# A channel product as seven products of block sums, with converted weights kept in DRAM

## The chip, the cores and the metric

The kernel runs on one core of a Trainium2 chip. Its time is the device time of one execution in microseconds (us). The engines are named as the profile names them: PE is TensorE's matmuls and PEld its weight loads, DVE is VectorE, ACT ScalarE, POOL GpSimd, SP SyncE. Each engine works through its own instructions in the order in which they are written; they wait for each other by semaphores.

## What is computed

```python
# attention with decay, 4 batches x 8 heads x 768 x 64, then a mixer
x = attn_out.transpose(0, 2, 1, 3).reshape(4, 768, 512)
h = relu(x.transpose(0, 2, 1) @ w_tok1) @ w_tok2       # tokens: 768 -> 256 -> 768
u = x + h.transpose(0, 2, 1)
out = u + relu(u @ w_ch1) @ w_ch2                      # channels: 512 -> 1536 -> 512
```

The mixer's weights come as 64-bit floats and are turned into 32-bit ones on the chip, by integer operations on the two words of each number. The change concerns the last line, `u @ w_ch1`, and what comes around it.

## The kernel before

*Attention stage (to some 185 us).* Sixteen pairs of heads run through a software pipeline; the mixer's token products are filled in between as "groups" (`token_hidden`, a tile `ph` of 18 matmuls, and `token_out`, a tile `pu` of 6), with weight conversions in the gaps. The result `u` lies transposed in SBUF, channels on partitions: 4 channel tiles by 3072 tokens.

*Channel stage.* The 3072 tokens are 6 blocks `k` of 512; the 1536 hidden channels are 6 groups `g` of 256. A unit is one (g, k). Each operand is split in a high and a low half of a reduced 32-bit format (`uh`/`ul`, `c1h`/`c1l`, `c2h`/`c2l`, `hh`/`hl`), and a product is three matmuls: high by high, low by high, high by low. `mm1` makes a hidden tile of 128 x 512 in PSUM from 4 channel tiles, 12 matmuls of 128x128 by 128x512 (L613). ACT takes its ReLU as the high half `hh` (L617), DVE subtracts for the low half `hl` (L618). `mm2` multiplies the two hidden tiles of a unit by the second weights, 6 matmuls for each of 4 output tiles (L634), and DVE adds the tile to `u` in place (L637). `mm2` runs one unit behind `mm1`, so PE alternates between the two. The blocks of `u` are split once, in the first six units (ACT L510, POOL L511).

*Order of the work.* It is written out by hand, instruction by instruction, for all five engines; no scheduler moves it. Small steps that fill gaps stand in a list `waiting`, and `later(n)` takes the next n of it. The conversion of a piece of weights (`narrow`) is such a list: an absolute value on ACT (L350), five steps on DVE (L351, L354, L357, L360, L363), a cast of the high half on ACT (L345), a subtraction of the low half on POOL (L346). A group has four pieces of 128x512. Group g+1 is loaded and converted during the six units of group g, one piece a unit.

PSUM has 8 banks: tag `sc` 4, `xT` 1, `sh` 3. At the end the last block is transposed by PE (L657) and written by two queues; the others by DVE (L644) and SP.

Of the kernel before, what the change touches and what calls it, by code (L numbers as in the profile page):

```python
# [21 lines left out]
def kernel(  # L22
# [310 lines left out]

    def narrow(raw, a, sg, hi, lo, view):

        low, high = raw[:, :, 0], raw[:, :, 1]
        af = a.bitcast(F32)

        def split():
            nc.scalar.copy(out=hi, in_=view(af))  # L345
            nc.gpsimd.tensor_sub(out=lo, in0=view(af), in1=hi.bitcast(F32))  # L346

        waiting.extend(
            [
                lambda: nc.scalar.activation(af, high.bitcast(F32), AF.Abs),  # L350
                lambda: nc.vector.tensor_scalar(  # L351
                    out=sg, in0=high, scalar1=0x80000000, scalar2=None, op0=ALU.bitwise_and
                ),
                lambda: nc.vector.scalar_tensor_tensor(  # L354
                    out=sg, in0=low, scalar=29, in1=sg, op0=ALU.logical_shift_right, op1=ALU.bitwise_or
                ),
                lambda: nc.vector.tensor_scalar(  # L357
                    out=af, in0=af, scalar1=HIGH_MIN, scalar2=HIGH_MAX, op0=ALU.max, op1=ALU.min
                ),
                lambda: nc.vector.tensor_scalar(  # L360
                    out=a, in0=a, scalar1=3, scalar2=0x40000000, op0=ALU.logical_shift_left, op1=ALU.bitwise_xor
                ),
                lambda: nc.vector.scalar_tensor_tensor(  # L363
                    out=a, in0=a, scalar=0x7FFFFFFF, in1=sg, op0=ALU.bitwise_and, op1=ALU.bitwise_or
                ),
                split,
            ]
        )
# [365 lines left out]
```

## Time and profile before

| | |
|---|---|
| median of 3 runs | 602.48 us (600.57 to 603.64) |
| profiled execution | 604.87 us, its span 603.1 us |
| granted TensorE clock, mean | 0.993 |
| matmuls | 3854, of which 864 in `mm1` and 864 in `mm2` |
| DRAM | read 34.61 MB, written 6.29 MB |

The span is counted from the first to the last instruction; what lies outside it (1.8 us here) is start and end of the execution. Busy time of an engine is time with an instruction in it; for PE, matmuls overlap each other, so that the length shown for one is more than the step from one to the next. A row of the groups reads: line, engine, operation, output <- inputs, shapes, xcount | busy us, mean ns of one | idle time of the engine ahead of it, and what ended it. The rows themselves stand in the prediction.

### The profile page before, as it was taken

The numbers are of one execution on the slowest core, as the hardware profiler recorded it, in microseconds if no ns is written. First come the engines' busy times: TensorE is split into PE (matmuls) and PEld (weight loads), VectorE is DVE, ScalarE is ACT, GpSimd is POOL, SyncE is SP. The second block draws the span as 40 slices with busy tenths as digits, with TensorE's granted clock in tenths as the row PEclk, the third lists the DMA queues.
The fourth block names the chain that finished last, engine by engine and source line by source line (L and its number), as shares of the span: only waits on it lengthen the run. The fifth ranks groups of instructions, "written<-read, shape, count | busy, mean of one in ns | idle before, by whom it ended". The sixth has DMA issues, their size and how long they took to land.

```text
span 603.1 us, 9441 instructions
## 1 busy us (share of the span) xinstructions
PE 581.8 (96%) x3854; PEld 493.9 (82%) x3854; DVE 327.0 (54%) x574; ACT 147.0 (24%) x283; POOL 162.0 (27%) x147
## 2 busy tenths in 40 slices
PE   5978899999999999999999999999999999999996
PEld 4877899989988878888888888888888888888885
DVE  4569867685552356635554356345553564445653
ACT  3344423343323123312121122111120121101101
POOL 6848655567613335400000011000010010000000
PEclk9979999999999999999999999999999999999999
DMA  9999696665101001100210101001110010006566
GB/s 185 242 226 168 103 189 134 136 115 92 30 34 36 2 35 36 41 30 36 69 36 0 36 35 38 33 1 65 41 35 1 35 36 1 1 4 101 83 102 130
DMA packets 142314, 41.50 MB, mean 69 GB/s; under 512 B 135104, under 2 KB 136640, under 8 KB 142272
## 3 DMA queue, kind: packets, MB, share of 16 engines
q1 hardware_dynamic: 141072, 40.12, 31.7%
q10 hardware_dynamic: 1200, 0.79, 0.4%
q8 instruction: 30, 0.49, 0.4%
q14 instruction: 12, 0.10, 0.1%
HBM read 34.61 MB, written 6.29 MB: 68 GB/s over the span
## 4 chain that ended last, share of the span: by engine, by line
PE 89%; DVE 5%; DMA 2%; ACT 2%; issue 1%; SPq 0%; DVEq 0%; ACTq 0%
PE ph L613 33%; PE po L634 33%; PE ph L419 6%; PE pu L439 5%; PE xT L285 3%; PE sc L261 3%; PE xT L295 2%; DMA uT<-in_moe_w_tok_dram 2%; PE kt L186 2%; PE kv L228 1%; PE xp L317 1%; DVE uT L354 1%; DMA qn<-in_q_dram 1%; DVE xlo L326 1%; DVE a L270 1%
## 5 line engine op out<-in xcount | busy, mean ns | idle before, releaser
L618 DVE SCALAR_TENSOR_TENSOR hl<-ph,hh 128x512 fp32r<-128x512 f32 x72 | 49.8, 692 | 189.5 <-ACT hh L617 189.5
L617 ACT ACTIVATE hh<-ph 128x512 fp32r<-128x512 f32 x72 | 43.1, 599 | 288.8 <-PE po L634 221.4
L613 PE MATMUL ph<-ul,c1h 128*128 128x512 f32 x288 | 113.4, 394 | 0.0
L613 PE MATMUL ph<-uh,c1l 128*128 128x512 f32 x288 | 113.2, 393 | 0.0
L613 PE MATMUL ph<-uh,c1h 128*128 128x512 f32 x288 | 113.1, 393 | 0.0
L634 PE MATMUL po<-hh,c2l 128*128 128x512 f32 x288 | 112.8, 392 | 0.0
L634 PE MATMUL po<-hh,c2h 128*128 128x512 f32 x288 | 112.8, 392 | 0.0
L634 PE MATMUL po<-hl,c2h 128*128 128x512 f32 x288 | 112.0, 389 | 0.0
L637 DVE TENSOR_TENSOR uT<-po,uT 128x512 f32<-128x512 f32 x144 | 95.7, 683 | 8.3 <-PE po L634 8.0
L613 PEld LDWEIGHTS ph<-ul,c1h 128*128 128x128 f32 x288 | 54.1, 188 | 12.3
L613 PEld LDWEIGHTS ph<-uh,c1h 128*128 128x128 f32 x288 | 54.2, 188 | 12.1
L634 PEld LDWEIGHTS po<-hh,c2h 128*128 128x128 f32 x288 | 54.0, 188 | 12.1
L634 PEld LDWEIGHTS po<-hl,c2h 128*128 128x128 f32 x288 | 54.1, 188 | 11.9
L613 PEld LDWEIGHTS ph<-uh,c1l 128*128 128x128 f32 x288 | 54.0, 188 | 11.9
L634 PEld LDWEIGHTS po<-hh,c2l 128*128 128x128 f32 x288 | 54.1, 188 | 11.5
L346 POOL TENSOR_TENSOR c1l<-wa,c1h 128x512 fp32r<-128x512 f32 x10 | 13.0, 1298 | 159.7 <-ACT c1h L345 159.7
L285 PE MATMUL xT<-a,vn 128*64 128x128 f32 x384 | 37.1, 285 | 6.3 <-ACT uT L302 6.3
L511 POOL TENSOR_TENSOR ul<-uT,uh 128x512 fp32r<-128x512 f32 x24 | 32.2, 1372 | 38.4 <-ACT uh L510 38.4
L346 POOL TENSOR_TENSOR c2l<-wa,c2h 128x512 fp32r<-128x512 f32 x10 | 13.0, 1302 | 91.7 <-ACT c2h L345 62.0
L210 POOL TENSOR_SCALAR kd<-kn,mask 128x320 f32<-128x320 f32 x32 | 36.5, 1151 | 1.3
L270 DVE TENSOR_TENSOR a<-sc,mask 128x384 f32<-128x384 f32 x64 | 31.3, 549 | 5.8 <-PE sc L261 5.6
L249 POOL COPY stb<-sv 64x320 f32<-64x320 f32 x32 | 26.1, 814 | 26.8 <-DVE sv L236 25.9
(76 smaller groups left out, 783.3 us busy)
## 6 DMA issues: line engine op xcount, KB each, us to landing
raw<-in_moe_w_ch_dram SPq DMA_DIRECT2D x20, 512.0 KB, 3.6
kn<-in_k_dram SPq DMA_DIRECT2D x32, 192.0 KB, 3.8
vn<-in_v_dram SPq DMA_DIRECT2D x16, 384.0 KB, 5.0
out_dram<-y SPq DMA_DIRECT2D x80, 64.0 KB, 2.0
qn<-in_q_dram SPq DMA_DIRECT2D x44, 96.0 KB, 3.8
uT<-in_moe_w_tok_dram SPq DMA_DIRECT2D x2, 1536.0 KB, 8.6
uT<-in_moe_w_ch_dram SPq DMA_DIRECT2D x4, 512.0 KB, 4.6
qn<-in_q_dram SPq DMA_DIRECT2D x10, 192.0 KB, 4.5
```

What stands on the lines that cost most here:

```text
L210: nc.gpsimd.tensor_scalar_mul(kds[i][:, h], loaded[i][0][:, 0 : NC - 1, h], mask[:, 2 * p + h, P - 1 : P])
L249: nc.gpsimd.tensor_copy(out=st[r, :, h, :], in_=sv[r].rearrange("p (e c) -> p c e", c=NC - 1))
L270: nc.vector.tensor_mul(out=a, in0=sc[h].rearrange("p (c i) -> p c i", i=P), in1=mask[:, 2 * p + h, None, :].broadcast_to([P, 3, P]),)
L285: nc.tensor.matmul(out=xT[h * D : (h + 1) * D, cs], lhsT=vns[i][:, h, c, :], rhs=weights_of[i, g, h][:, cg, :], start=(cg == 0), stop=False,)
L419: nc.tensor.matmul(out=ph, lhsT=w[:, c, fs], rhs=x[:, c], start=(i == 0), stop=(i == 3 * NC - 1))
L439: nc.tensor.matmul(out=pu, lhsT=h[:, kk, cs], rhs=w[:, kk, ss], start=(i == 0), stop=(i == 3 * NK - 1))
L511: nc.gpsimd.tensor_sub(out=two(ul[:, t]), in0=ub, in1=two(uh[:, t]).bitcast(F32))
L613: nc.tensor.matmul(out=ph, lhsT=w[:, ct, js], rhs=x[:, ct], start=(i == 0), stop=(i == 11))
L617: nc.scalar.activation(hh, ph, AF.Relu)
L618: nc.vector.scalar_tensor_tensor(out=hl, in0=ph, scalar=0.0, in1=hh.bitcast(F32), op0=ALU.max, op1=ALU.subtract)
L634: nc.tensor.matmul(out=po, lhsT=w[:, jj, cs], rhs=h, start=(i == 0), stop=(i == 3 * JG - 1))
L637: nc.vector.tensor_add(out=ub, in0=two(po), in1=ub)
```

## The change

`u @ w_ch1` is done for pairs of blocks by Winograd's form of the 2x2 scheme: token blocks 2r and 2r+1 (top, bot), the two halves of the 512 input channels, and the two halves of a group's 256 hidden channels make eight products of 128-wide hidden tiles, which become seven products of sums. A *quad* n is a pair r and a group g: n = 6r + g, so the channel stage is three passes (r = 0, 1, 2) over the six groups, 18 quads.

- Weights: `combine` builds four sums of the converted quarters on POOL, then splits seven operands in halves (ACT `high`, POOL `low`), the last four as one operation of 128x1024.
- Tokens: three operands are plain (`raw_operand`: 1, 2, 3), four are sums (`make` on DVE, `part` splits them on ACT and POOL or DVE: 6, 7, 5, 4). For the first pass operands 1 and 2 are made in the attention stage, the others in quad 0, each right ahead of its product. For later passes they are made in the last quad of the pass before, after the old operand's last product.
- Products (`PROD`: order 1, 2, 6, 7, 5, 3, 4, six matmuls each) accumulate into three banks `a`, `b`, `d`. Bank `b` collects products 1, 6, 5, 3, and ACT takes snapshots of it on the way (`snap`); DVE adds a snapshot to `a` or `d` (`whole`), and `relu` takes the sum. In the first five quads three of four ReLUs go the "slow" way: a second ReLU in place on ACT, and the subtraction on POOL instead of DVE.
- `mm2` of quad n-1 is done between the products of quad n, one output tile after each of six products and two after the seventh; it now uses the `sh` banks. In quad 0 the remaining ten token groups take that place; the units used to mix with the last ones of these.
- Group g+1 is converted during quad g of the first pass (four pieces in one quad). The converted halves are written to DRAM (`keep_c1`, `keep_c2`, SP queue) and fetched for passes 1 and 2, the first weights a quad ahead, the second in the quad itself, a quad ahead of their `mm2`.
- The last block to finish is 4, not 5.

```diff
@@ weights of a group
+        return [
+            lambda: eng.tensor_add(out=s1, in0=a0[:, :, 1], in1=a1[:, :, 1]),
+            raw0,
+            lambda: eng.tensor_sub(out=s2, in0=s1, in1=a0[:, :, 0]),
+            lambda: eng.tensor_sub(out=s3, in0=a0[:, :, 0], in1=a0[:, :, 1]),
+            raw1,
+            lambda: eng.tensor_sub(out=s4, in0=a1[:, :, 0], in1=s2),
+            sums,
+        ]
...
+    PROD = (1, 2, 6, 7, 5, 3, 4)
+    WI = {1: 0, 2: 1, 4: 2, 5: 3, 6: 4, 7: 5, 3: 6}
...
+    def halve(r, o, ct, src, eng):
+        oh, ol = ops[r, o]
+        nc.scalar.copy(out=two(oh[:, ct]), in_=src)
+        eng.tensor_sub(out=two(ol[:, ct]), in0=src, in1=two(oh[:, ct]).bitcast(F32))
...
+        terms = {
+            1: lambda ct: (block(bot, ct), block(top, ct)),
+            2: lambda ct: (block(bot, 2 + ct), two(tt[1][:, ct])),
+            3: lambda ct: (block(bot, 2 + ct), block(bot, ct)),
+            4: lambda ct: (block(top, 2 + ct), two(tt[2][:, ct])),
+        }
...
+            6: [
+                lambda: make(1, 0, V),
+                lambda: make(1, 1, V),
+                lambda: make(2, 0, V),
+                lambda: part(6, 2, 0, G),
+                lambda: make(2, 1, V),
+                lambda: part(6, 2, 1, V),
+            ],
+            7: [lambda: make(3, 0, V), lambda: part(7, 3, 0, G), lambda: make(3, 1, V), lambda: part(7, 3, 1, V)],
+            5: [lambda: part(5, 1, 0, G), lambda: part(5, 1, 1, V)],
+            3: raw_operand(r, 3, ob, G),
+            4: [lambda: make(4, 0, V), lambda: part(4, 4, 0, G), lambda: make(4, 1, V), lambda: part(4, 4, 1, V)],
...
+        nc.scalar.activation(hh, src, AF.Relu)
+        if slow:
+            nc.scalar.activation(src, src, AF.Relu)
+            nc.gpsimd.tensor_sub(out=hl, in0=src, in1=hh.bitcast(F32))
...
@@ mm1, now product(n, s)
+        into = {1: "b", 2: "a", 6: "b", 7: "d", 5: "b", 3: "b", 4: "d"}[o]
...
-        for ct in range(4):
-            for w, x in ((c1h, uh), (c1l, uh), (c1h, ul)):
-                nc.tensor.matmul(out=ph, lhsT=w[:, ct, js], rhs=x[:, ct], start=(i == 0), stop=(i == 11))
+        for ct in range(2):
+            for w, x in ((ch, oh), (cl, oh), (ch, ol)):
+                nc.tensor.matmul(
+                    out=c[into], lhsT=w[:, WI[o], ct], rhs=x[:, ct], start=(first and i == 0), stop=(i == 5),
...
+        slow = r == 0 and g < NG - 1
...
+        if o == 1:
+            snap("p1")
+        elif o == 2:
+            relu(n, 0, 0, whole("a", "p1"), slow)
+        elif o == 6:
+            snap("u2")
+        elif o == 5:
+            snap("u4")
+            relu(n, 1, 1, whole("d", "u4"), slow)
+        elif o == 3:
+            relu(n, 0, 1, c["b"], False)
+        elif o == 4:
+            relu(n, 1, 0, whole("d", "u2"), slow)
...
@@ the loop over quads
+            if n == 0:
+                for f in steps.pop(o, []) if o > 2 else []:
+                    f()
...
+            if r == 0 and g < NG - 1:
+                if s == 2:
+                    convert(g + 1, 0)
+                if s == (4 if n == 0 else 2):
+                    convert(g + 1, 1)
...
+                if s == 6:
+                    convert(g + 1, 2)
+                    convert(g + 1, 3)
...
+                if n + 1 < NQD and n + 1 >= NG:
+                    fetch_c1(n + 1)
+                if n >= NG:
+                    fetch_c2(n)
+            product(n, s)
+            later(4 if n == 0 and s >= 5 else 2)
+            if n == 0:
+                for _ in range(plan.get(s, 0)):
+                    rest.pop(0)()
                     later(1)
...
+            else:
+                for q_ in range(s, s + 1 if s < 6 else 8):
+                    mm2(n - 1, 1 - q_ // 4, q_ % 4)
+                    flush()
+                    later(2)
+            flush()
+            if nxt:
+                for f in nxt[o]:
+                    f()
```

How this stands on the engines, at three places. The digits in a name are its group, block or quad and a running number; `uT` is `u`, `pu` a token group's output tile, `tt` a sum of token blocks, `o6h`/`o6l` operand 6 in halves, `xu`/`xp` a sum of `whole`, `sm` the weight sums.

DVE where the channel stage begins, before:

```order
L424 SCALAR_TENSOR_TENSOR hl3_2360<-ph311_2499,hh3_2359 128x256
L618 SCALAR_TENSOR_TENSOR hl2001_2534<-ph2001_2520,hh2001_2533 128x512
L444 TENSOR_TENSOR uT_60<-pu300_2537,uT_60 128x384
L444 TENSOR_TENSOR uT_60<-pu310_2545,uT_60 128x384
L618 SCALAR_TENSOR_TENSOR hl2010_2577<-ph2010_2563,hh2010_2576 128x512
L637 TENSOR_TENSOR uT_60<-po000_2588,uT_60 128x512
```

DVE at the same place, now (quad 0, up to operand 6):

```order
L427 SCALAR_TENSOR_TENSOR hl3_2373<-ph311_2497,hh3_2372 128x256
L740 TENSOR_TENSOR xp10_2536<-a0_2529,p10_2474 128x512
L447 TENSOR_TENSOR uT_60<-pu300_2543,uT_60 128x384
L447 TENSOR_TENSOR uT_60<-pu310_2551,uT_60 128x384
L660 TENSOR_TENSOR tt01_2559<-uT_60 128x512 x2
L660 TENSOR_TENSOR tt02_2562<-uT_60,tt01_2559 128x512 x2
L539 TENSOR_TENSOR o6l0_2565<-tt02_2562,o6h0_2564 128x512
```

Behind the adds of two token tiles there now stand the four subtractions and a low half on which product 6 waits.

ACT during the conversion of group 3, before (units of group 2):

```order
L350 ACTIVATE wa30_3480<-raw30_3479 128x512
L617 ACTIVATE hh2211_3603<-ph2211_3590 128x512
L345 CAST c1h3_3475<-wa30_3480 128x512
L617 ACTIVATE hh2220_3644<-ph2220_3631 128x512
L350 ACTIVATE wa31_3550<-raw31_3549 128x512
L617 ACTIVATE hh2221_3681<-ph2221_3668 128x512
```

ACT at the end of quad 2, now, and into quad 3:

```order
L493 CAST c1h3_3087<-wa31_3021 128x2x2x128
L493 CAST c1h3_3087<-sm3_3023 128x1024
L696 ACTIVATE hh021_3140<-xu22_3138 128x512
L698 ACTIVATE xu22_3138<-xu22_3138 128x512
L347 ACTIVATE wa32_3124<-raw32_3067 128x512
```

The cast of the weight sums `sm` now stands ahead of the ReLUs of product 4 and of the next piece's absolute value.

POOL during the conversion of group 3, before:

```order
L346 TENSOR_TENSOR c1l3_3476<-wa30_3480,c1h3_3475 128x512
L346 TENSOR_TENSOR c1l3_3476<-wa31_3550,c1h3_3475 128x512
L346 TENSOR_TENSOR c2l3_3478<-wa32_3628,c2h3_3477 128x512
L346 TENSOR_TENSOR c2l3_3478<-wa33_3706,c2h3_3477 128x512
L346 TENSOR_TENSOR c1l4_3924<-wa40_3928,c1h4_3923 128x512
```

POOL there now:

```order
L509 TENSOR_TENSOR sm3_3023<-wa30_3019,wa31_3021 128x256
L489 TENSOR_TENSOR c1l3_3088<-wa30_3019,c1h3_3087 128x256
L511 TENSOR_TENSOR sm3_3023<-sm3_3023,wa30_3019 128x256
L512 TENSOR_TENSOR sm3_3023<-wa30_3019 128x256
L489 TENSOR_TENSOR c1l3_3088<-wa31_3021,c1h3_3087 128x2x2x128
L514 TENSOR_TENSOR sm3_3023<-wa31_3021,sm3_3023 128x256
L489 TENSOR_TENSOR c1l3_3088<-sm3_3023,c1h3_3087 128x1024
```

The two low halves of the first weights have become seven operations, of which the first needs both converted pieces.

More of the change, by code (lines that the diff above doesn't have):

```diff
@@ L311, in turn_back @@
             x_of[b, half] = [
-                tokp.tile([P, NC, DM // 2], F32R, tag=t, bufs=2, name=f"{t}{b}{half}") for t in ("xhi", "xlo")
+                tokx.tile([P, NC, DM // 2], F32R, tag=t, bufs=2, name=f"{t}{b}{half}") for t in ("xhi", "xlo")
             ]
@@ L346, in split @@
             nc.gpsimd.tensor_sub(out=lo, in0=view(af), in1=hi.bitcast(F32))
[L348 to L368, printed above, removed]
+        return [split]
     def words(b):
@@ new lines, in convert_piece, with combine, low, high @@
+    def convert_piece(raw, a, sg):
+        return narrow(raw.rearrange("p (n two) -> p n two", two=2), a, sg)
+    def combine(n, pool, a0, a1, s, eng):
+        a0, a1 = (x.bitcast(F32).rearrange("p (t w j) -> p t w j", t=2, w=2) for x in (a0, a1))
+        s1, s2, s3, s4 = (s[:, w] for w in range(4))
+        def low(sl, src, perm):
+            hi, lo = c1s[n]
+            lo, hi = lo[:, sl], hi[:, sl].bitcast(F32)
+            if perm:
+                lo, hi = lo.rearrange("p w t j -> p t w j"), hi.rearrange("p w t j -> p t w j")
+            nc.gpsimd.tensor_sub(out=lo, in0=src, in1=hi)
+        def high(sl, src, perm):
+            hi = c1s[n][0][:, sl]
+            nc.scalar.copy(out=hi.rearrange("p w t j -> p t w j") if perm else hi, in_=src)
+        def raw0():
+            c1_tiles(n, pool())
+            high(0, a0[:, :, 0], False)
+            low(0, a0[:, :, 0], False)
+        def raw1():
+            high(slice(1, 3), a1, True)
+            low(slice(1, 3), a1, True)
+        def sums():
+            high(slice(3, 7), s, False)
+            low(slice(3, 7), s, False)
+        return [
+            lambda: eng.tensor_add(out=s1, in0=a0[:, :, 1], in1=a1[:, :, 1]),
[5 more added lines that the diff above has]
+            sums,
+        ]
@@ new lines, with sums_of, make, part @@
+    op_ = {1: oa, 2: oa, 3: ob, 4: ob, 5: ob, 6: ob, 7: ob}
+    tp = ctx.enter_context(tc.tile_pool(name="tp", bufs=1, reuse_waits="tile"))
+    p3 = ExitStack()
+    dr = ctx.enter_context(tc.tile_pool(name="dr", bufs=1, space=bass.MemoryType.DRAM))
+    yp_ = wb = hp = wp = None
+    def sums_of(r):
+        top, bot = 2 * r, 2 * r + 1
+        tt = {}
+        terms = {
[4 more added lines that the diff above has]
+        }
+        def make(n, ct, eng):
+            if ct == 0:
+                tt[n] = tp.tile([P, 2, CB], F32, tag="tt", bufs=3, name=f"tt{r}{n}")
+            x, y = terms[n](ct)
+            eng.tensor_sub(out=two(tt[n][:, ct]), in0=x, in1=y)
+        def part(o, n, ct, eng):
+            if ct == 0:
+                operand(r, o, op_[o])
+            halve(r, o, ct, two(tt[n][:, ct]), eng)
+        return make, part
@@ new lines, in fetch_c1, with fetch_c2, raw_of @@
+    def fetch_c1(n):
+        c1_tiles(n, wb if n % 2 else wa)
+        for d, w in zip(kept[n % NG, 1], c1s[n]):
+            nc.sync.dma_start(out=w.rearrange("p w t j -> p (w t j)").bitcast(F32), in_=d)
+    def fetch_c2(n):
+        c2_tiles(n, wb if n % 2 else wa)
+        for d, w in zip(kept[n % NG, 2], c2s[n]):
+            nc.sync.dma_start(out=w.rearrange("p j e -> p (j e)").bitcast(F32), in_=d)
+    fresh = {}
+    def raw_of(g, i):
+        fresh[g, i] = wp.tile([P, 1024], U32, tag="raw", bufs=2, name=f"raw{g}{i}")
+        load_piece(g, i, fresh[g, i])
```

326 lines of the change are left out of this document (194 added, 132 removed).

## The prediction

> **What bounds the kernel now.** I read the header of the page, then the busy time by stage, then the chain of waits, then the groups of instructions, then the timeline of VectorE (DVE) and GpSimd (POOL) around the weight conversion. Header and stages (columns: window, its length, then busy time and instruction count of PE, PEld, DVE, ACT, POOL, then the granted TensorE clock, DMA share, GB/s):
>
> ```profile
> span 603.1 us, 9441 instructions
> PE 581.8 (96%) x3854; PEld 493.9 (82%) x3854; DVE 327.0 (54%) x574; ACT 147.0 (24%) x283; POOL 162.0 (27%) x147
> 185.40:204.70 19.30, 19.30 (x108) 17.31 (x108) 6.18 (x11) 6.99 (x14) 8.46 (x7) 1.00 0.01 1
> 218.20:259.80 41.60, 41.60 (x181) 33.81 (x181) 25.29 (x40) 15.08 (x27) 20.95 (x15) 1.00 0.15 51
> 391.90:591.00 199.10, 199.10 (x870) 162.96 (x869) 101.41 (x168) 30.96 (x52) 10.40 (x8) 1.00 0.21 40
> ...
> 259.78 2.72 PE ph L613 x12
> 262.50 2.72 PE po L634 x12
> ...
> 292.42 2.81 PE ph L613 x12
> 295.23 2.76 PE po L634 x12
> ```
>
> From 185 us on TensorE never idles: its busy time equals the window. A matmul is therefore worth its pitch, not its shown duration of 0.39. The four rows of the chain give (2.72 + 2.72 + 2.81 + 2.76) / 48 = 0.2294 us. The other engines are half idle, so today nothing they do is seen.
>
> **What is saved.** The first product has 72 tiles of 12 matmuls, 864. After it has 18 quads (a pair of token blocks by a weight group) of 7 products of 6 matmuls, 756. 108 x 0.2294 = 24.8 us less. The second product keeps 864. A quad has 42 + 48 = 90 matmuls, 20.6 us. Whether the saving is seen depends on the other engines keeping 20.6 us a quad, so I price those next.
>
> ```profile
> L637 DVE TENSOR_TENSOR uT<-po,uT 128x512 f32<-128x512 f32 x144 | 95.7, 683 | 8.3 <-PE po L634 8.0
> L617 ACT ACTIVATE hh<-ph 128x512 fp32r<-128x512 f32 x72 | 43.1, 599 | 288.8 <-PE po L634 221.4 <-PE ph L613 67.4
> L444 DVE TENSOR_TENSOR uT<-pu,uT 128x384 f32<-128x384 f32 x32 | 17.6, 554 | 12.0 <-PE pu L439 12.0
> L510 ACT CAST uh<-uT 128x512 fp32r<-128x512 f32 x24 | 13.2, 619 | 0.0
> L350 ACT ACTIVATE wa<-raw 128x512 f32<-128x512 f32 x20 | 13.2, 658 | 0.0
> L346 POOL TENSOR_TENSOR c1l<-wa,c1h 128x512 fp32r<-128x512 f32 x10 | 13.0, 1298 | 159.7 <-ACT c1h L345 159.7
> L215 POOL TENSOR_TENSOR qs<-qT,lamp 128x640 f32<-128x640 f32 x16 | 24.9, 1554 | 0.0
> L173 POOL COPY keep<-lamp 128x256 f32<-128x256 f32 x4 | 1.4, 397 | 3.2 <-DVE lamp L168 3.2
> 188.14 4.31 PE ph L419 x36
> ...
> 195.21 2.09 PE pu L439 x12
> ```
>
> DVE instructions that follow each other start closer than they last; this stretch of one conversion shows the pitch (start, length, engine):
>
> ```profile
> 292.24 0.69 DVE L618 SCALAR_TENSOR_TENSOR hl<-ph,hh 128x512 fp32r<-128x512 f32 x1 [4.10 <-ACT hh L617]
> 292.85 0.42 DVE L360 TENSOR_SCALAR wa<-wa 128x512 uint32<-128x512 uint32 x1
> 293.30 0.69 DVE L363 SCALAR_TENSOR_TENSOR wa<-wa,ws 128x512 uint32<-128x512 uint32 x1
> 293.91 1.28 DVE L637 TENSOR_TENSOR uT<-po,uT 128x512 f32<-128x512 f32 x2
> 296.57 0.42 DVE L351 TENSOR_SCALAR ws<-raw 128x512 uint32<-128x512 uint32 x1
> 296.90 0.69 DVE L637 TENSOR_TENSOR uT<-po,uT 128x512 f32<-128x512 f32 x1
> ```
>
> So 0.61 for an operation that reads two tensors, 0.45 for a one-input step that another waits for, 0.33 for the first. A converted piece is five steps, 0.33 + 0.61 + 0.45 + 0.45 + 0.61 = 2.45. A POOL sum of 128x256, new here, has no row: 0.40 if it were the copy, 0.65 as half of 1.30, 0.79 on the slope from 512 to 640; I take 0.75, since the nearest rows are two-input ones. A cast of 1024 on ACT is taken at 1.17.
>
> **First quad (n=0).** Its operands for products 6, 7, 5, 3, 4 are built right before each product, and nothing else stands on PE there. PE's own work is 42 matmuls, two hidden tiles and eight output tiles: 9.6 + 4.3 + 8.4 = 22.3. The waits, each from the last PE work ahead:
> - Product 6: DVE adds the last output tile 0.55, three subtractions 1.9, ACT casts 0.62, POOL subtracts 1.30, then four matmuls 0.9. 5.3, less its own 1.4, and handovers: 4.1 lost.
> - Product 7: add 0.55, a conversion step 0.45, one subtraction 0.6, cast 0.62, POOL 1.30, 0.9: 3.3 lost.
> - Product 5: one DVE add and one subtraction: 0.3.
> - Product 3: its low halves stand on POOL behind the weight sum of group 1, which needs DVE's conversion, which needs ACT's third step. From the end of product 5: snapshot 0.60, sum 0.68, two ReLUs and an absolute value 1.86, four DVE steps 2.1, POOL 0.75 + 1.30 + 1.30, last matmul 0.23: 8.8, less two output tiles (2.1) and its own 1.4: 5.4.
> - Product 4: behind five POOL operations, 0.60 + 0.35 + 0.75 x 3 + 1.30 x 2, then 0.9: 6.7 less 1.4, 5.4.
>
> 18.5 in all. Ends 14 (the cheap POOL sum, one wait of 3 covered) and 21.
>
> **Rest of pass 1 (n=1 to 4).** Before, a group is converted over four of six units of 11 us (259.78 to 292.42 holds three); now over one quad of 20.6. By the pitches DVE has 11 sums or adds, one subtraction (12 x 0.61) and four conversions (9.8), 17.1 of 20.6, so the sum fits. The order closes a loop: DVE's third step waits for ACT's absolute value; ACT has that behind the ReLUs of product 4 and, ahead of those, the cast of the weight sums; the cast waits for five POOL sums and halves; the first waits for the last DVE step of the second piece, and POOL has a ReLU's half ahead of it. One turn: DVE's 18 conversion steps 8.9, five adds 3.05, two sums 1.3; ACT's two ReLUs 1.2; POOL 1.30 + 4 x 0.75 + 1.30 + 0.75; ACT 1.17 + 0.6 + 0.6 + 0.66. It makes 23.8, with handovers 24. PE needs 20.6, so it waits.
> Second, DVE and POOL block each other:
>
> ```profile
> 219.95 5.70 POOL L511 TENSOR_TENSOR ul<-uT,uh 128x512 fp32r<-128x512 f32 x4 [13.61 <-ACT uh L510]
> 220.39 1.41 DVE L354 SCALAR_TENSOR_TENSOR ws<-raw,ws 128x512 uint32<-128x512 uint32 x1
> 222.32 0.92 DVE L357 TENSOR_SCALAR wa<-wa 128x512 f32<-128x512 f32 x1
> 297.50 0.68 DVE L354 SCALAR_TENSOR_TENSOR ws<-raw,ws 128x512 uint32<-128x512 uint32 x1
> ```
>
> The same step takes 1.41 beside POOL and 0.68 alone, and POOL's four take 5.70 where four of 1.30 make 5.2. In DVE's part of the loop stand four POOL operations, 5.2 us. I take 2 of these as added: 26 a turn; ends 24 (nothing) and 28. The Trainium skill, SBUF — State Buffer, "Who interferes with whom", goes further: a DVE instruction with two SBUF inputs or in a two-port mode and a POOL instruction that reads SBUF exclude each other for the whole instruction. By that rule the turn could reach 24 + 5.2 = 29.2 and the total 13 us more than mine; the 1.41 agrees with it, but half of DVE's work there reads PSUM.
> From the end of product 4 of n=0: 6.0 to the first absolute value (sum, two ReLUs, POOL 1.30 + 0.75, cast, absolute value), four turns less 0.6, and 1.6 to the end of product 6 of n=5: 111.0. PE's own is 4 x 20.6 + 6.9 = 89.3. Lost 21.7; ends 13.7 and 29.7.
>
> **Between passes.** In n=5 the next pass's operands are built. ACT holds the snapshot after product 5 behind the casts for operands 6 and 7, and these wait for DVE's subtractions, which stand behind what is left of the conversion. Counted from ACT's last-but-one absolute value, DVE has eight conversion steps 4.0, five adds 3.05, a sum 0.6, six subtractions 3.7, two halves 1.2 with a cast of 0.62 ahead of one; then ACT's casts and snapshot 1.2: the snapshot is done at 14.5 while POOL works all along, where product 3 could start at 8.5. 7 lost, ends 3 and 10. In n=11 no conversion is left: 2.5, ends 1 and 4. Quads 6 to 10 and 12 to 17 have 15 DVE operations, some 9.2 of 20.6, and lose nothing.
>
> **TensorE's clock.** It drops after a gap (the window's columns as above):
>
> ```profile
> 33.00:36.00 3.00, 0.02 (x2) 0.02 (x2) 2.97 (x8) 1.00 (x2) 0.37 (x1) 0.84 1.24 230
> 36.00:39.00 3.00, 3.00 (x25) 2.67 (x26) 2.69 (x4) 0.14 (x1) 3.00 (x3) 0.50 0.85 161
> 39.00:42.00 3.00, 3.00 (x16) 3.00 (x16) 0.00 (x0) 2.17 (x6) 2.84 (x4) 0.52 1.05 189
> ```
>
> An idle of 3.1 us is followed by 6 us at half rate, about 3 us lost. The waits of n=0 are pieces of 2.5 to 3.3, so at most some trip it: 2, ends 0 and 8.
>
> **Kept weights.** A quad fetches 2 x 128 x (1792 + 1024) x 4 bytes, 2.88 MB, a quad ahead.
>
> ```profile
> raw<-in_moe_w_ch_dram SPq DMA_DIRECT2D x20, 512.0 KB, 3.6
> 20.00:30.00 10.00, 10.00 (x135) 8.53 (x135) 5.10 (x10) 4.98 (x12) 8.06 (x8) 1.00 0.96 263
> ```
>
> At the 146 GB/s of one transfer alone (512 KB in 3.6) that is 19.8 us, at 263 GB/s 11: hidden in 20.6. SyncE's queue holds the 16 or 32 result writes of n=6 and n=12 only behind fetches due earlier. In the attention stage POOL gets four sums more, 3 us: 0.5, ends 0 and 2. If operand addresses make all 1620 matmuls of the faster or the slower pitch, -4.4 or +4.4; I take 0.
>
> **Sum.** -24.8 + 18.5 + 21.7 + 7 + 2.5 + 2 + 0.5 = +27.4. The profiled execution took 604.87 (span 603.1), 2.4 above the median of 602.48: 629.9, so 630. All low ends give +2.5 (605 beside the median), all high ends +54 (657).
>
> **Rivals.**
> - Other side, 12%: the loop doesn't close, since the absolute values are done before the sums' cast is due. For it: DVE's 17.1 fits in 20.6, and the waits of n=0 are the only long ones. Pass 1 then costs 0, and with 18.5 in n=0, 3 and 1 between passes the total is 600; if n=0 also hides all but 5, it is 581. It decides once all losses stay under 24.8. Against it: ACT's order.
> - The clock, 5%: the Trainium skill, TensorE: Matmul & The Clock Gate, "HAM oscillation", says that gaps of some 3.4 us let the clock fall again. As a mechanism here: each of the four long waits in n=0 costs the 3 us of the row above (+12, 640), and if waits in every turn keep PE at half rate, a quad needs 41 instead of 26: four times 15, 690.
> - Late fetches, 3%: 3 us in each of 12 quads, 666. Against it: the 263 GB/s.
> - That 7 products aren't 7 is excluded: the PE order has 756 matmuls there.
>
> **Chances.** My forecast 80%; mostly slower. Same means within 0.5%, 3 us, which is what a measurement of this kernel can tell: 599.5 to 605.5. It holds 5%: the low end of my forecast and the upper case of the other side. Faster 11%, slower 84%. The range 604 to 650 leaves out the other side and part of the clock and fetch cases.
>
> **What would show it.** Right: PE's chain with pieces of ACT, DVE and POOL between 185 and 330 us; n=0 near 43 us, the next four quads near 26, quads 6 to 10 at 20.6 with PE never idle; the conversion's second step on DVE (L354 before, another line after) with a mean well above the 0.68 of the row without POOL. Wrong: PE full from 185 on, as before; or waits on DMA for c1h at each quad's start.

## The result, and the profile after

The changed kernel takes 663.89 us (median of 4 runs, 662.4 to 665.0) where the kernel before takes 603.06 in the same comparison: ratio 1.101, 95% interval 1.0965 to 1.1057. The forecast was slower, 630 within 604 to 650; the direction came true, the size did not: +61 where I had +27.

Header of the page after, then, from the view by windows, busy time by stage (columns as in the prediction). The stages are: two stretches of the attention stage, quad 0, quads 1 to 4, quad 5, and two stretches of passes 2 and 3.

```profile
span 661.4 us, 9534 instructions
```
```profile
100.00:130.00 30.00, 26.14 (x284) 23.69 (x283) 19.22 (x35) 9.42 (x20) 17.94 (x17) 0.89 0.47 102
...
192.40:240.20 47.80, 29.99 (x129) 23.78 (x128) 25.14 (x36) 13.72 (x25) 15.84 (x13) 0.78 0.14 45
240.20:352.50 112.30, 93.28 (x361) 72.78 (x360) 85.97 (x128) 44.13 (x76) 54.48 (x46) 0.90 0.47 178
352.50:390.60 38.10, 26.63 (x92) 20.45 (x92) 28.81 (x35) 14.81 (x26) 22.85 (x17) 0.82 0.44 165
400.00:500.00 100.00, 100.00 (x435) 81.45 (x434) 51.93 (x78) 21.64 (x36) 2.54 (x2) 1.00 0.49 162
520.00:640.00 120.00, 120.00 (x522) 97.71 (x521) 64.56 (x97) 26.04 (x43) 1.30 (x1) 1.00 0.42 137
```

TensorE is full again in passes 2 and 3, quad after quad at 20.7 us: the saving is there. All losses lie before 391 us and in quad 11. By the starts of product 1 in the timeline of PE:

| part | own length or before | after | lost | forecast |
|---|---|---|---|---|
| start of the first channel product | 185.2 | 192.5 | 7.3 | 0.5 |
| quad 0 | 22.3 | 47.8 | 25.5 | 18.5 + 2 (clock) |
| quads 1 to 4, and quad 5 to the end of product 6 | 89.3 | 126.4 | 37.1 | 21.7 |
| rest of quad 5 | 13.7 | 23.8 | 10.1 | 7 |
| quad 11 | 20.7 | 23.8 | 3.1 | 2.5 |
| 108 matmuls fewer | | | -24.8 | -24.8 |

The sum is 58.3, the difference of the spans (661.4 - 603.1).

One turn of pass 1, from the timelines of POOL, DVE, ACT and PE one after the other (start, length, engine, line, operation; in brackets the idle time ahead and what ended it):

```profile
269.46 0.72 POOL L514 TENSOR_TENSOR sm<-wa,sm 128x256 f32<-128x256 f32 x1
271.35 2.38 POOL L489 TENSOR_TENSOR c1l<-sm,c1h 128x1024 fp32r<-128x1024 f32 x1 [1.16 <-ACT c1h L493]
...
273.12 0.90 DVE L354 TENSOR_SCALAR wa<-wa 128x512 f32<-128x512 f32 x1 [5.56 <-ACT wa L347]
274.05 1.37 DVE L357 TENSOR_SCALAR wa<-wa 128x512 uint32<-128x512 uint32 x1
...
277.11 1.65 DVE L351 SCALAR_TENSOR_TENSOR ws<-raw,ws 128x512 uint32<-128x512 uint32 x1
...
284.37 1.33 DVE L354 TENSOR_SCALAR wa<-wa 128x512 f32<-128x512 f32 x1 [0.21 <-ACT wa L347]
...
289.50 0.69 DVE L360 SCALAR_TENSOR_TENSOR wa<-wa,ws 128x512 uint32<-128x512 uint32 x1
...
301.82 0.89 DVE L354 TENSOR_SCALAR wa<-wa 128x512 f32<-128x512 f32 x1 [4.88 <-ACT wa L347]
...
270.22 1.05 ACT L493 CAST c1h<-sm 128x1024 fp32r<-128x1024 f32 x1 [5.56 <-POOL sm L514]
...
272.37 0.65 ACT L347 ACTIVATE wa<-raw 128x512 f32<-128x512 f32 x1
276.22 0.62 ACT L369 CAST c2h<-wa 128x512 fp32r<-128x512 f32 x1 [3.21 <-issue]
276.75 0.67 ACT L347 ACTIVATE wa<-raw 128x512 f32<-128x512 f32 x1
277.32 0.56 ACT L736 COPY p<-b 128x512 f32<-128x512 f32 x1
...
271.99 0.39 PE L771 MATMUL po<-hl,c2h 128*128 128x512 f32 x1
277.94 0.79 PE L727 MATMUL b<-o6h,c1h 128*128 128x512 f32 x1 [5.56 <-ACT p L736]
278.53 0.63 PE L727 MATMUL b<-o6h,c1l 128*128 128x512 f32 x1
278.96 0.63 PE L727 MATMUL b<-o6l,c1h 128*128 128x512 f32 x1
```

DVE stands 5.56 us until the absolute value (L347 at 272.37), which ACT has behind the cast of the sums (L493 at 270.22), and this waited 5.56 for POOL's last sum: the loop of the forecast. DVE's steps then last 1.37 and 1.65 where they take 0.42 and 0.69 alone (rows of s1 below). There is also a wait that the forecast lacks: ACT's snapshot `p`, ready to be taken since product 1, stands behind the cast of `c2h`, which waits for DVE's steps on that piece, and behind one more absolute value. `c1l` is whole at 273.73 (271.35 + 2.38), but product 6 starts at 277.94, and then at half rate (0.43 from one matmul to the next).

### The profile page after: what moved, and what is told of

Read it like the earlier page. It is cut to its first block, busy times and chain, and to the rows that moved or that the text cites. A ratio compares the mean times of both kernels' runs of the same rounds, so it can differ in the third digit from the quotient of the medians.

```text
span 661.4 us, 9534 instructions
## 1 busy us (share of the span) xinstructions
PE 584.0 (88%) x3746; PEld 486.3 (74%) x3746; DVE 416.1 (63%) x649; ACT 201.4 (30%) x376; POOL 220.9 (33%) x198
## 5 line engine op out<-in xcount | busy, mean ns | idle before, releaser
L774 DVE TENSOR_TENSOR uT<-po,uT 128x512 f32<-128x512 f32 x144 | 98.8, 687 | 86.3 <-PE po L771 85.2
L696 ACT ACTIVATE hh<-xu 128x512 fp32r<-128x512 f32 x36 | 22.7, 632 | 80.2 <-PE po L771 47.7
L736 ACT COPY u<-b 128x512 f32<-128x512 f32 x36 | 21.0, 584 | 83.8 <-PE b L727 83.7
L727 PE MATMUL b<-o6h,c1h 128*128 128x512 f32 x36 | 17.3, 482 | 25.2 <-ACT p L736 21.4
L251 POOL COPY stb<-sv 64x320 f32<-64x320 f32 x32 | 26.1, 816 | 35.4 <-DVE sv L238 34.5
L740 DVE TENSOR_TENSOR xu<-d,u 128x512 f32<-128x512 f32 x36 | 24.8, 688 | 18.3 <-ACT u L736 14.0
L304 ACT COPY uT<-xT 128x384 f32<-128x384 f32 x32 | 15.3, 477 | 61.4 <-PE xT L297 61.4
L354 DVE TENSOR_SCALAR wa<-wa 128x512 f32<-128x512 f32 x20 | 16.4, 821 | 26.1 <-ACT wa L347 26.1
L297 PE MATMUL xT<-qs,stb 128*64 128x128 f32 x320 | 32.2, 278 | 0.0
L287 PEld LDWEIGHTS xT<-a,vn 128*64 128x64 f32 x384 | 23.3, 141 | 10.1 <-ACT uT L304 7.0
L328 DVE TENSOR_TENSOR xlo<-xp,xhi 128x384 fp32r<-128x384 f32 x32 | 17.6, 554 | 19.4 <-ACT xhi L327 19.3
L422 PE MATMUL ph<-xhi,w1h 128*128 128x256 f32 x96 | 28.3, 295 | 1.7 <-DVE uT L447 1.3
```

Source lines behind the costliest of these rows:

```text
L251: nc.gpsimd.tensor_copy(out=st[r, :, h, :], in_=sv[r].rearrange("p (e c) -> p c e", c=NC - 1))
L287: nc.tensor.matmul(out=xT[h * D : (h + 1) * D, cs], lhsT=vns[i][:, h, c, :], rhs=weights_of[i, g, h][:, cg, :], start=(cg == 0), stop=False,)
L297: nc.tensor.matmul(out=xT[h * D : (h + 1) * D, cs], lhsT=st[:, c - 1, h, :], rhs=qss[i][:, c - 1, :], start=False, stop=(cg == 2),)
L422: nc.tensor.matmul(out=ph, lhsT=w[:, c, fs], rhs=x[:, c], start=(i == 0), stop=(i == 3 * NC - 1))
L696: nc.scalar.activation(hh, src, AF.Relu)
L727: nc.tensor.matmul(out=c[into], lhsT=w[:, WI[o], ct], rhs=x[:, ct], start=(first and i == 0), stop=(i == 5), skip_group_check=True,)
```

## The experiments

Times are medians, and the kernel before took 602.9 to 603.9 beside them; "turn" is the time from one quad's product 1 to the next one's. In the changed kernel the turns of quads 1 to 4 are 26.1, 29.8, 28.0 and 28.4, and quad 5 takes 38.0.

**Which part of the change, and which theory.**

*e1*: quad 0's operands emitted sooner.
```diff
-                for f in steps.pop(o, []) if o > 2 else []:
-                    f()
...
+            if n == 0:
+                for early_o in {0: (6,), 1: (7,), 2: (5, 3), 3: (4,)}.get(s, ()):
+                    for f in steps[early_o]:
+                        f()
```


> Only the first quad's operand steps are emitted sooner: those of product 6 behind product 1, of 7 behind 2, of 5 and 3 behind 6, of 4 behind 7; the same steps on the same engines. Order theory (the engines' queues hold the operand chains behind the ReLUs and output tiles): the quad's excess over its own 22.3 us falls from 25.5 us to 6 to 10 us, with it the granted clock in it rises from 0.77 to above 0.9, and the time falls to 645 to 650 us. Engine-time theory (the chains simply take DVE, ACT and POOL longer than the products before them last): the excess falls by no more than 5 us, 659 us or more. Traffic theory (the DRAM transfers slow the pass): no change, 664 us.

647.68 us. Quad 0 took 28.3 in place of 47.8, its clock 0.94; quad 1 gave 2.4 back (28.5). So most of quad 0's loss, 19.5 of 25.5, was the place of the steps in the queues, not their length.

*e3*: two weight groups for all.
```diff
-            if r == 0 and g < NG - 1:
+            if r == 0 and 0 < g < NG - 1 and s == 0:
+                c1s[g + 1], c2s[g + 1] = c1s[(g + 1) % 2], c2s[(g + 1) % 2]
+            if r == 0 and g == 0:
```


> Only weight groups 0 and 1 are loaded and converted; later groups of pass 1 use these two again, so the output isn't the reference's. Stores to DRAM and fetches from it stay as they are. Order theory (the pass-1 turn is the chain through one scratch tile and three in-order engines): turns of quads 1 to 4 fall from 26 to 30 us back to 20.6 us, the 37.1 us of pass 1 go, and part of the 10.1 us of quad 5: 620 to 627 us. Traffic theory (stores and fetches are what slow it): 655 us or more, since only the loads go. Clock theory (the half rate behind the first quad's gaps is carried through pass 1): quads 1 to 4 stay near 25 us, 645 us.

624.50 us; turns 23.1, 20.8, 20.7, 20.8, quad 5 25.3. Without the later conversions pass 1 runs at PE's pace. The half rate of quad 0 isn't carried on.

*e4*: no keep and no fetch.
```diff
-                if r == 0:
-                    keep_c1(g)
...
+                    c1s[n], c2s[n] = c1s[4 + n % 2], c2s[4 + n % 2]
```


> Neither stores of converted weights to DRAM nor fetches of them: passes 2 and 3 use the tiles of groups 4 and 5 in turn, so the output isn't the reference's. Order theory: nobody waits for these transfers, 664 us within 1.5 us. Traffic theory (DRAM and SBUF traffic of 69 MB read and 24 MB written slows the engines): tens of us less, below 645 us.

664.54 us, quad by quad as the changed kernel (turns 27.7, 28.1, 28.0, 28.5). The stores and fetches cost nothing that shows; that theory falls.

*e6*: PE kept busy in its waits.
```diff
+            warm(n, {2: 14, 3: 9, 5: 7, 6: 10}.get(s, 0) if n == 0 else 24 if s == 2 and 2 <= n < NG else 0)
             product(n, s)
```


> Matmuls into a PSUM bank that nobody reads stand where PE waits: 14, 9, 7 and 10 ahead of products 6, 7, 3 and 4 of the first quad, 24 ahead of product 6 in quads 2 to 5 (136 in all, 31 us of PE time placed in waits). Clock theory (the half rate behind the gaps lengthens the path): the granted clock in the first quad rises from 0.77 to above 0.95, the quad loses 5 to 8 us, the turns up to 1 us each: 650 to 659 us. Rival (the half rate lies beside waits on the other engines and costs nothing): 664 us, or a few us more where the added matmuls outlast a wait.

663.11 us. The clock rose, the time stayed (quad 0 and quads 1 to 4):

```profile
192.60:237.90 45.30, 37.18 (x168) 29.84 (x167) 25.16 (x36) 13.72 (x25) 15.95 (x13) 0.91 0.14 47
237.90:350.40 112.50, 104.83 (x433) 80.58 (x432) 85.50 (x128) 44.14 (x76) 54.69 (x46) 0.99 0.47 178
```

Quad 0 gained 2.5, quads 1 to 4 nothing (112.5 where they took 112.3 at 0.90). In the turn from 264.0 us on, the added matmuls end at 275.44 and the snapshot that product 6 needs at 275.52, so they hold nothing up; product 6 then runs at full rate, and the turn is 28.8 all the same. In pass 1 the half rate lies beside chains on other engines: the rival held.

*e7*: group 0's sums spread over the attention stage.
```diff
+                waiting.extend(both[:4] if i == 8 else both[4:6])
...
+        if i == 10:
+            waiting.append(both[6])
```


> Group 0's weight sums in the attention stage are spread: the first four steps one pair of heads later, the next two a pair later still, the wide cast and its low half two more later; pieces 2 and 3 convert in a tile of their own. Order theory (ACT's and POOL's in-order queues held the attention's own steps behind the sums): the first channel product starts at 185 to 188 us in place of 192.5, 657 to 660 us. Rival (the 4.7 us more of POOL work are on the path wherever they stand): 190 us or later, 662 us or more.

656.54 us; the first product starts at 185.1. The edit also gives pieces 2 and 3 of group 0 a tile of their own, since the spread steps still read the old one; the two aren't told apart. PE's window 100 to 130 us is full as before the change, 29.72 at clock 1.00 (kernel e7, then the kernel before):

```profile
100.00:130.00 30.00, 29.72 (x370) 27.75 (x367) 22.25 (x40) 11.31 (x25) 16.18 (x17) 1.00 0.61 124
```
```profile
100.00:130.00 30.00, 29.66 (x370) 27.45 (x367) 21.00 (x42) 11.89 (x26) 18.75 (x18) 1.00 0.65 132
```

In the changed kernel ACT's timeline shows the attention's own cast (L327) last in a queue:

```profile
120.30 1.05 ACT L493 CAST c1h<-s0early 128x1024 fp32r<-128x1024 f32 x1 [1.70 <-POOL s0early L514]
121.25 0.65 ACT L347 ACTIVATE uT<-uT 128x512 f32<-128x512 f32 x1
121.81 0.46 ACT L327 CAST xhi<-xp 128x384 fp32r<-128x384 f32 x1
```

*e8*: the next pass's operands two products later.
```diff
+            lag.append(nxt[o] if nxt else [])
+            for f in lag.popleft():
```


> In quads 5 and 11 the steps that build the next pass's operands are emitted two products later (those of product 6 behind product 5, and so on, the last two in the next quad). Order theory (the snapshot behind product 5 stands on ACT behind casts that wait for DVE): quad 11's 3.1 us fall to 1 or less, quad 5's 10.1 us behind product 6 by 3 to 6 us: 656 to 661 us. Rival (DVE and POOL have too much to do there, whatever the order; the steps then delay quad 6 or 12): 663 to 666 us.

656.53 us: quad 5 38.0 to 29.2, quad 11 23.8 to 20.7, but quads 6 and 12 rose from 20.8 to 23.3, since product 5 waits there for the snapshot behind product 6, and this now stood on ACT behind operand 4's casts. Net 6.3 and 0.6.

**The turn: order or sharing.**

*e5*: absolute values first.
```diff
+                waiting.extend([a2, a3, fresh[g, "sums"]] + r2 + r3 + [s2, s3])
```


> One change of order in pass 1: ACT's absolute values of a group's third and fourth piece stand ahead of the cast of the weight sums, and the casts of these two pieces behind both their DVE steps. Same work. Loop theory (the turn of 28.4 us is the chain DVE first half, POOL sums, ACT cast, ACT absolute value, DVE second half, with DVE idle some 5.5 us a turn): turns fall to 22 to 25 us and the time to 637 to 650 us. Throughput theory (DVE and POOL with their mutual blocking are simply full in a turn): turns stay above 27.5 us, 660 us or more.

649.75 us, turns 25.2, 26.2, 26.2, 26.3. The loop is cut, yet the turn falls by 2 and not by 4 to 6: DVE, idle 4.1 to 5.6 at this place in each turn before, is now busy 93.4 of 103.9 us, and PE waits for POOL's `c1l` (7.4 us ahead of product 6 in four quads). Each theory had half. Not all that the edit gives is in these turns: they give 8.4, quad 0 gives 3.7 (44.1) and quad 5 2.8 (35.2), while quad 11 takes 1.6 more.

*e2*: the low halves of the hidden layer on DVE.
```diff
-        slow = r == 0 and g < NG - 1
+        slow = False
```


> In pass 1 the hidden layer's low halves all go to DVE; the second ReLU on ACT and the POOL subtraction that three of the four had are gone (15 fewer on each, 15 more steps on DVE). Blocking theory (DVE's conversion steps are stretched by POOL's subtractions, 1.37 and 1.65 us where they took 0.42 and 0.61): with 0.73 us x3 of POOL work out of each turn and 0.6 us x3 more on DVE, a turn loses 1 to 2 us or stays level, 652 to 662 us. Traffic theory: no change, 664 us. If DVE's own work were the bound of the turn and POOL did not matter, 1.8 us more in each of four turns: 670 us.

650.46 us, turns 23.2, 27.4, 26.7, 25.8: 15 steps more on DVE and a faster pass, below even the 652 that was expected at best. So DVE's own work wasn't the bound. Whether it is POOL's time that counted isn't shown by this run alone: the edit also takes the second ReLU off ACT, some 0.6 us a turn ahead of the absolute value.

*s2*: the weights' low halves left out (a second cast on ACT stands in their place), the order untouched.
```diff
-            nc.gpsimd.tensor_sub(out=lo, in0=src, in1=hi)
+                nc.scalar.copy(out=lo, in_=src)
```


> The changed kernel with the weights' low halves of groups 1 to 5 as plain casts on ACT in place of POOL's subtractions, its order untouched; the output isn't the reference's. My forecast's loop without blocking was 24 us a turn. If the loop alone sets the turn and the stretch is its second part: POOL's wide step and its neighbours leave the loop (some 1.3 us between sums, 2 more of stretch), turns of 24 to 25.5 in place of 28.4, 640 to 650 us. If the sharing was all of it: 21 to 22 us, 625 to 632 us. If the order alone was: 27.5 us or more, 658 us or more.

647.85 us, turns 24.5, 27.3, 25.9, 27.3 (mean 26.3 for 28.1). The first of the three, in time; the mean turn is above its 25.5. Three of the new casts (256, 512 and 1024 wide, 0.39 + 0.61 + 1.05 us by their high halves' casts) stand on ACT, where the loop runs, which may be why this edit doesn't reach the 24; no run tests that.

*b1*: the changes of e1 (with operand 4 ahead of 3), e2, e5, e7 and a variant of e8 together.


> All the changes of order together: the first quad's operands early (4 ahead of 3), low halves on DVE, absolute values first, group 0's sums spread in the attention stage, the next pass's operands one to two products later. Theory (in-order queues, then the sharing between DVE and POOL): attention 7 us back, first quad at 28 us (20 back), turns near 24 us (16 to 20 back), quad 5 some 9 to 12 back, quad 11 some 3 back: 600 to 608 us. If the gains overlap (a turn freed of one wait falls into the next): 615 to 625 us.

620.58 us: the second case. The single gains, 16.2 + 13.4 + 14.1 + 7.4 + 7.4, make 58.5; together they are 43.3. Quads 6 and 12 took 27.5 and 26.1.

*b3*: b1 with the weight sums on DVE (`combine(..., nc.vector)`).


> As the other kernel of this call, with the four weight sums of groups 1 to 5 on DVE in place of POOL (four times 0.73 us of POOL a turn become DVE work of about 0.4 us each). Sharing theory (DVE's steps on SBUF wait for whole POOL instructions, so POOL time is DVE time): a turn falls by 1 to 2 us against the other kernel, 4 to 9 us in all. Rival (DVE is full by its own work, POOL only overlaps): a turn rises by 1.6 us, 6 to 8 us slower than the other.

624.62 us, slower by 4: neither 4 to 9 less nor quite 6 to 8 more. What is taken from POOL isn't won when DVE gets it.

*b5*: b1 with operands 5, 3, 4 of the next pass built in the next quad.
```diff
+            pace = {2: 2, 3: 2, 4: 6, 5: 4} if nxt else {0: 2, 1: 2, 2: 4}
```


> As the kernel with all orders (620.6 us), but the operands of products 5, 3 and 4 for the next pass are built in the next quad, behind its products 1, 2 and 6. There quads 6 and 12 took 27.5 and 26.1 us, since the snapshot of product 1 stood on ACT behind casts of operands 5 and 3, and product 2's sum on DVE behind operand 4. Order theory: both fall to 21 to 23 us, 610 to 614 us. Rival (that work has no room anywhere near): it moves the wait to products 5 to 4 of quads 6 and 12, 617 to 622 us.

614.84 us; quads 6 and 12 24.8 and 22.4: between the two expectations.

*s1*: b5 with s2's edit.


> As the other kernel of this call, but the low halves of the weights of groups 1 to 5 are plain casts on ACT in place of POOL's subtractions, so the output isn't the reference's: 6.9 us of POOL work a group go (0.73, 1.28, 2.35, two of 1.29), 3.3 us of ACT work come. Sharing theory (DVE's SBUF steps wait for whole POOL instructions): DVE's conversion steps come down to 0.42 and 0.69 us, turns of quads 1 to 4 fall from some 26 to 21 to 23.5 us, 12 to 22 us less in all. Rival (DVE is full by its own work, POOL merely overlaps): turns stay within 0.5 us, 3 us less at most.

594.57 us, 20.3 less than b5; turns 22.4, 21.3, 21.1, 21.3 for 26.9, 27.5, 27.0, 25.6. The groups of DVE, 245 to 345 us, show where it was (line, operation, count | busy us, mean ns | idle; changed kernel, then b5, then s1):

```profile
L774 DVE TENSOR_TENSOR uT<-po,uT 128x512 f32<-128x512 f32 x27 | 18.3, 682 | 1.5 <-PE po L771 1.4
L351 DVE SCALAR_TENSOR_TENSOR ws<-raw,ws 128x512 uint32<-128x512 uint32 x15 | 15.9, 1058 | 0.4
L357 DVE TENSOR_SCALAR wa<-wa 128x512 uint32<-128x512 uint32 x15 | 9.8, 652 | 0.4
```
```profile
L357 DVE TENSOR_SCALAR wa<-wa 128x512 uint32<-128x512 uint32 x14 | 12.9, 919 | 0.2
L351 DVE SCALAR_TENSOR_TENSOR ws<-raw,ws 128x512 uint32<-128x512 uint32 x13 | 11.9, 919 | 0.4
```
```profile
L781 DVE TENSOR_TENSOR uT<-po,uT 128x512 f32<-128x512 f32 x37 | 25.1, 681 | 1.9 <-PE po L778 1.8
L351 DVE SCALAR_TENSOR_TENSOR ws<-raw,ws 128x512 uint32<-128x512 uint32 x12 | 8.3, 692 | 0.4
L357 DVE TENSOR_SCALAR wa<-wa 128x512 uint32<-128x512 uint32 x12 | 5.1, 422 | 0.2
```

From b5 to s1 the steps L351 and L357 fall from 919 each to 692 and 422 (1058 and 652 in the changed kernel); the sum that takes one input from PSUM (L774, L781) has 682 and 681 beside POOL and without. DVE's busy time in quads 1 to 4 falls from 97.1 to 79.8, by 17.3 of the 20.8 that the four turns lose. This is shown: POOL's work on SBUF is paid in DVE's time. It isn't the whole 20.8, since PE's waits for POOL's `c1l`, 3.6 in b5, go as well. And not every step pays: L360, also with two inputs in SBUF, has 692 in b5 and 693 in s1; why, no run tells.

**A version worth having.**

*b6*: b5 with the weights' low halves on DVE (`nc.vector`), a step or two behind their casts; as there are more steps, three in place of two are taken at each place in pass 1.


> As the kernel with later operands (614.8 us), with the weights' low halves of groups 1 to 5 on DVE in place of POOL, each a step or two behind its cast (3.4 us of DVE a group come, 6.9 us of POOL go), the weight sums stay on POOL. Sharing theory: turns of quads 1 to 4 go from 27 to 23.5 to 25 us, 600 to 607 us. Rival (DVE's own load is the bound): turns of 28 us or more, 620 us or more.

613.71 us, 1.1 less: both missed. Quad 0 and the turns take 30.0, 29.4, 24.8, 23.2 and 24.8, where b5 has 28.4, 26.9, 27.5, 27.0 and 25.6: the later turns win what the first ones lose. DVE's steps are short (422, 690), but it now waits for ACT's casts, 8.5 us in five groups:

```profile
L489 DVE TENSOR_TENSOR c1l<-wa,c1h 128x256 fp32r<-128x256 f32 (+1 forms) x10 | 8.7, 875 | 4.0 <-ACT c1h L493 4.0
L489 DVE TENSOR_TENSOR c1l<-sm,c1h 128x1024 fp32r<-128x1024 f32 x5 | 6.1, 1226 | 4.5 <-ACT c1h L493 4.5
```

*b7* and *b8*: two pieces' steps alternate on DVE; b7 on b6, b8 on b5.
```diff
+            waiting.extend([a0, absolute] + [f for two_ in zip(r0, rest_of) for f in two_])
```


> As the kernel with the low halves on DVE, and two pieces' steps alternate on DVE, so that no step follows the one whose result it reads (0.45 us from start to start where it does, 0.33 where not, three times a piece): up to 1.4 us a turn less, 594 to 604 us; if blocking by POOL covers this, the same time as the other.

> As the kernel with later operands, its low halves on POOL, with two pieces' steps alternating on DVE: up to 1.4 us a turn less, 608 to 612 us; if POOL's instructions set DVE's pace, 614 to 616 us as without.

610.19 and 604.53 us. b7 gains 3.5 on b6, between its two expectations. b8 gains 10.3 on b5, 1.5 to 4 a turn (25.4, 24.1, 22.8, 22.9), more than the 1.4 of the shorter steps; why more, no run tells apart. Against the kernel before: 1.003 (1.0004 to 1.0058).

*b9*: b8 with operand 4's halves behind product 7 in quad 0, and operand 7 built in quad 6 or 12. *b10*: b9 with three conversion steps in place of two at each place.


> As the kernel with two pieces abreast and low halves on POOL (604.5 us), with the halves of the first quad's operand 4 built behind product 7 in place of product 6, and operand 7 of the next pass built in the next quad behind its first product. Order theory: the first quad falls from 28.4 to 25 to 27 us, quad 6 from 25.4 to 22 to 24: 598 to 603 us. Rival (DVE is full there, any order gives the same): 604 to 606 us.

> As the other kernel of this call, with three conversion steps in place of two at each place in quads 1 to 5. If quad 1's wait for the weight sums (25.4 us in place of 20.7) comes from steps emitted late: 2 to 3 us less than the other. If DVE is the bound of the turn: the same within 1.5 us, or slower, since output-tile sums then stand behind more conversion.

609.29 and 601.94 us. b9, slower than its rival's 604 to 606, won 2.2 in quad 0 and 1.2 in quad 2 and lost 1.8, 2.3 and 1.5 in quads 1, 6 and 12: waits moved, and to worse places. Another 2.0 lie ahead of the first product (186.7 for 184.7 us, by the same instructions), a spread between executions that is in every small difference here. In b10 quad 1 was 26.1 for 27.2, less than the 2 to 3 expected, and quads 2 to 5 fell by about a microsecond each (21.7, 21.6, 21.8, 20.7); its first product started at 182.4, so of the 10.0 between the two profiled executions 4.3 aren't the edit's. Against the kernel before b10 is 0.998 (0.9949 to 1.0013): no difference. So the seven products, in the best of these orders, only come back to the old time. No kernel tried is faster than the one before with its work intact.

## Why the prediction was right or wrong

The sum was +27.4, and the spans differ by 58.3. Of the 30.9 between, 15.4 lie in the rest of pass 1, 6.8 in the attention stage, 5.0 in quad 0, 3.1 in quad 5 and 0.6 in quad 11.

*Right.* The saving (quads of 20.7 from 391 us on), the fetches hidden (e4), the loop through ACT's order in pass 1 (e5, and DVE's 5.56 us idle), quad 11 (3.1 for 2.5), and the direction.

*Rest of pass 1, 37.1 for 21.7: the blocking, 2 a turn, was mis-sized, and the exit was wrong.* The forecast's 111.0 were 5.4 to the start of the first absolute value, 104 for four turns and 1.6 from there to the end of product 6 of quad 5. By the starts of these absolute values (245.61 and 358.44) they took 5.3, 112.8 and 8.3.

The turns of the loop were 26.8 and three times 28.7, where I had 24 without blocking and 2 for it. The trace of a turn has 17.0 us from DVE's L354 at 273.12 to the end of its last step at 290.1, against 13.3 by pitches. Four steps stretched beside POOL make 3.3 of it: from start to start 0.93, 1.40, 1.57 and 1.36, where 0.45, 0.45, 0.61 and 0.45 were taken. POOL's and ACT's part, up to L354 at 301.82, took 11.7 against 10.6. So a turn stood 4.7 above the 24, beyond the upper end that I had (28), and the four turns cost 8.8 more than forecast. The Trainium skill, SBUF — State Buffer, "Who interferes with whom", which gave 29.2 a turn, was nearer than my discount; the rows of L774 and L351 agree with its distinction between PSUM and SBUF inputs. My discount argued that half of DVE's work reads PSUM. By the forecast's own terms it is a third in DVE's part of the loop (five adds and two sums, 4.35 of 13.25), and the steps that were stretched beside POOL are those that don't.

The other 6.7 are the exit: I had product 6 of quad 5 follow `c1l` directly, with one matmul left (POOL, ACT and PE in quad 5; the last line is product 3, for the paragraph on quad 5):

```profile
357.42 2.36 POOL L489 TENSOR_TENSOR c1l<-sm,c1h 128x1024 fp32r<-128x1024 f32 x1 [1.16 <-ACT c1h L493]
...
358.44 0.65 ACT L347 ACTIVATE wa<-raw 128x512 f32<-128x512 f32 x1
...
363.99 0.79 PE L727 MATMUL b<-o6h,c1h 128*128 128x512 f32 x1 [5.54 <-ACT p L736]
...
381.00 0.79 PE L727 MATMUL b<-o3h,c1h 128*128 128x512 f32 x1 [5.93 <-ACT u L736]
```

`c1l` is whole at 359.78, and product 6 starts 4.2 later, behind ACT's snapshot; its six matmuls then take 2.7 at half rate, where I had 0.23 for the last one. Of ACT I had asked only what stands ahead of the absolute value, not what stands ahead of the snapshot. In e5, which puts the casts of `c2h` behind DVE's steps on both pieces, PE has no wait for `p` in quads 1 to 5.

*Quad 0, 25.5 for 20.5.* PE's waits in it (view of the waits, 192 to 241 us: who, for what, us in total, times, longest):

```profile
PE b L727 <- ACT o6h L538: 3.8, 1, 3.8
PE b L727 <- POOL o3l L539: 3.4, 1, 3.4
PE d L727 <- ACT o4h L538: 3.0, 1, 3.0
PE d L727 <- POOL o4l L539: 2.7, 1, 2.7
PE d L727 <- ACT o7h L538: 2.3, 1, 2.3
PE b L727 <- ACT o3h L538: 1.7, 1, 1.7
PE d L727 <- POOL o7l L539: 0.6, 1, 0.6
```

They are 17.5 in all, and product by product near the forecast: 3.8, 2.9, 0, 5.1 and 5.7, where I had 4.1, 3.3, 0.3, 5.4 and 5.4. What failed is the clock term of 2: the other 8.0 are PE's own work, some 30 at a granted 0.78 where I had 22.3, the upper end of the term (8). What the clock costs the quad is less than that. In e6, at 0.91, PE's own work falls by 4.3 (29.9 to 25.6), the waits, with the added matmuls in them, grow by 1.9, and the quad is 2.5 shorter. So part of the half rate lies beside the chains, and the forecast's waits, counted beside a PE at full rate, came out near partly by luck: with a faster PE they are longer. What a clock of 1.00 would give, no run shows.

*Attention stage, 7.3 for 0.5: the step that failed outright.* I counted POOL's 3 us of sums as work in gaps and didn't ask what stood behind them: ACT's queue held the attention's own cast (L327) behind the cast of the sums, as the row above shows. Such queues I followed in the channel stage alone. e7 gave the 7.4 back by moving the seven steps of these sums, with the tile that this takes.

*Quad 5, 10.1 for 7*: just above its upper end of 10; the snapshot behind the casts, as named (PE waits 5.93 for it, the row at 381.00). e8, which moves these steps, takes 8.8 off quad 5 and adds 2.5 to quad 6. *The rivals*: "other side" was excluded by the loop; late fetches cost nothing; the clock rival's first part, 12 us in quad 0, was nearer to the 8.0 than my 2; its 690 needed half rate in every turn on the path, and e6 shows that in pass 1 it lies off the path. *The range*: even all upper ends together gave only +54. I had taken the terms as independent guesses, but 14.1 of the 30.9 that they missed (4.2 at the exit, 6.8 and 3.1) have one cause, instructions that stand in an in-order queue behind one that waits. Three terms (attention stage, pass 1, quad 5) passed their upper ends together.

## What to carry to other kernels

When a change takes work from a full engine and gives three others more, list for each of the others what stands *behind* every new instruction that waits, in every stage that it touches, and add these: here 83 us of losses came for 24.8 saved, and other places for the steps, with fifteen low halves moved from POOL to DVE, took 49 of them off again (b5). Count POOL's SBUF time as DVE's where DVE's steps have all their operands in SBUF: 6.9 us of POOL a group cost 5.2 a turn, of which 4.3 were DVE's busy time. Idle time of a queue isn't free room: DVE was idle for 23% of quads 1 to 4 and for 10% as soon as the loop was cut (e5), while the turns fell by only 2 us.
